# A blocked forward substitution turned the other way round: one 32 by 32 product for each pair of blocks, three sets per slot instead of four

## The chip, the core and the metric

The kernel runs on one core of one Trainium2 chip. The metric is the device time of one execution in microseconds (us), given as the median of several executions. All executions told of here are on record as in the fast state. A ratio between two kernels is the mean time of one kernel's fast runs over the mean of the other's of the same rounds, so it is not quite the ratio of the medians that are quoted.

## The reference

Attention of the delta-rule kind for 4 batches, 8 heads, 768 tokens and 48 columns a head; its output, brought to 3072 rows of 384, goes through an MLP of 2048 hidden columns. Everything is fp32. `beta` is between 0.1 and 0.4.

```python
k_n = k / (np.linalg.norm(k, axis=-1, keepdims=True) + 1e-06)
for t in range(S):
    kt, vt, bt = (k_n[:, :, t], v[:, :, t], beta[:, :, t, None])
    y[:, :, t] = np.einsum('bhd,bhde->bhe', q[:, :, t], state)
    v_old = np.einsum('bhde,bhd->bhe', state, kt)
    state = state + bt[:, :, :, None] * np.einsum('bhd,bhe->bhde', kt, vt - v_old)
...
x = np.ascontiguousarray(attn_out.transpose(0, 2, 1, 3)).reshape(B * S, H * D)
h = x @ w_in
return (h * (1.0 / (1.0 + np.exp(-1.702 * h)))) @ w_out
```

## The kernel before

The 768 steps are done in 6 chunks of 128 tokens, so that there are 24 *units*, one for each chunk and batch. In a unit, the values that the state really takes up (U) come from a lower triangular system of 128 rows for each head. It is solved in four blocks of 32 rows. The diagonal blocks have been inverted beforehand by VectorE (XB). Block b is then `U[b] = XB[b] * (V[b] - sum over a < b of G[a,b]^T U[a])`, where V holds the values and G comes from the products of the unit's keys with each other. The kernel forms each sum by *one* product over all blocks above, so its rows of the array are 32, 64 or 96, and calls it psR:

```python
def keys(self):                      # V -= what the state holds for these keys
    ...
    psK = [bank("psK", (128, NP, D)) for _ in range(2)]
    ...                              # 8 products
    for hh in range(2):
        Vh = self.V[:, hh::2, :]
        vec.tensor_tensor(Vh, Vh, psK[hh], op=ALU.subtract)

def above(self, blk, h, psR):
    r, a = slice(blk * BS, (blk + 1) * BS), slice(0, blk * BS)
    pe.matmul(psR[r, h, :], lhsT=self.G[a, h, 0, r], rhs=self.U[a, h, :], start=True, stop=True)

def rest(self, blk, psR):            # VectorE
    r = slice(blk * BS, (blk + 1) * BS)
    vec.tensor_tensor(self.V[r], self.V[r], psR[r], op=ALU.subtract)

def solve(self, blk, h, psU):
    r = slice(blk * BS, (blk + 1) * BS)
    pe.matmul(psU[r, h, :], lhsT=self.XB[r, h, :], rhs=self.V[r, h, :], start=True, stop=True)

def solved(self, blk, psU):          # ScalarE
    r = slice(blk * BS, (blk + 1) * BS)
    act.copy(self.U[r], psU[r])
```

`slot(n)` works on three units at once, A (unit n-1), B_ (unit n) and D_ (unit n+1), in six groups. Between the groups it puts MLP matmuls (ph, po), which need nothing from these units and fill TensorE. psR, psU, psK, psY (queries and outputs) and psS (state) come from one pool of four PSUM buffers, which `bank` hands out in turn:

```python
if group == 0:    psR of A, block 2
elif group == 1:  psU of A, block 2, mixed head by head with psR of B_, block 1
elif group == 2:  psR of A, block 3;  D_ begins: D_.keys()
elif group == 3:  psU of A block 3, B_ block 1, D_ block 0;  A.queries()
elif group == 4:  A.state()
else:             A.outputs()
# after each group: some instructions of the inversion (VectorE), weight conversion, MLP
```

(The cases are told in words here; the code is in the diff below.)

## Time and profile before

| | before |
|---|---|
| time, median of 3 (range) | 853.62 us (852.58 to 853.96) |
| span of the profiled execution | 851.5 us |
| TensorE busy | 93% |
| VectorE busy | 57% |
| sets of substitution products in a steady slot | 4 (16, 32, 16 and 48 matmul records) |
| one steady slot | 31.1 us |

The main views stand in the prediction. What it does not show are the page's groups of the instructions that the change touches. The columns are line, engine, operation, output and inputs, shapes and count; then busy time in us and mean ns of one; then the engine's idle time ahead of them and what ended it.

```profile
L529 DVE TENSOR_TENSOR V<-V,psR 32x384 f32<-32x384 f32 x68 | 37.6, 553 | 92.5 <-PE psR L522 91.4
L522 PE MATMUL psR<-US,G 64*32 64x48 f32 (+2 forms) x1088 | 60.8, 207 | 0.0
L533 PE MATMUL psU<-V,XB 32*32 32x48 f32 x1424 | 42.5, 204 | 2.3 <-DVE V L529 2.3
```

The "+2 forms" are the products over 32, 64 and 96 rows. The mean of 207 ns is the length of one record; the 1088 of them make 60.8 us of busy time, so they overlap for the most part, and 207 ns is not what one costs. A group is not complete either, because the first slots' instructions carry the line of a helper.

### The profile page before, as it was taken

How to read it: one execution, taken by the hardware profiler on the slowest of the kernel's cores; microseconds unless marked ns; L12 is line 12 of the kernel's file. 1: busy time of each engine (PE TensorE's matmuls, PEld its weight loads, DVE VectorE, ACT ScalarE, POOL GpSimd, SP SyncE). 2: the span in 40 equal slices, each digit the busy share in tenths (PEclk: the TensorE clock that was granted, in tenths of full speed). 3: DMA queues.
4: the chain of work that ended last, by engine and by line, in shares of the span. 5: the costliest groups of instructions: out<-in, count | busy, mean ns of one | idle time of the engine just before them, and what ended most of it. 6: DMA issues, size and time to landing. Idle time of an engine off the chain costs nothing.

```text
span 851.5 us, 16186 instructions
## 1 busy us (share of the span) xinstructions
PE 794.0 (93%) x6884; PEld 578.7 (68%) x6884; DVE 483.2 (57%) x1025; ACT 200.8 (24%) x383; POOL 106.0 (12%) x120
## 2 busy tenths in 40 slices
PE   8308898899999999999999999999999999999998
PEld 7206677656766867867767767767767768677684
DVE  5799869978993592582682672772762840110100
ACT  3202544232311312312212312213212112112020
POOL 2102321231021202102102101101100000000000
PEclk9658969999999999999999999999999999999999
DMA  9798653451322213223122132032032020000000
GB/s 150 157 158 152 162 143 81 112 142 34 77 59 58 60 42 73 54 64 69 36 66 68 36 85 57 18 86 54 10 79 52 1 58 2 10 15 1 24 1 18
DMA packets 160967, 55.80 MB, mean 66 GB/s; under 512 B 128672, under 2 KB 157568, under 8 KB 160896
## 3 DMA queue, kind: packets, MB, share of 16 engines
q1 hardware_dynamic: 154048, 46.02, 26.6%
q0 software_dynamic: 1856, 7.87, 3.0%
q10 hardware_dynamic: 4992, 0.89, 0.9%
q8 instruction: 54, 0.88, 0.4%
q14 instruction: 17, 0.14, 0.1%
HBM read 33.13 MB, written 20.45 MB: 63 GB/s over the span
## 4 chain that ended last, share of the span: by engine, by line
PE 78%; DVE 12%; DMA 6%; issue 2%; POOL 1%; ACT 0%; ACTq 0%; SPq 0%; DVEq 0%; POOLq 0%
PE po L629 28%; PE ph L614 27%; PE psG L368 4%; PE psR L522 4%; PE psY L549 4%; PE psU L533 4%; PE psK L512 2%; DVE P L104 2%; DMA w_out<-in_moe_w_out_dram 2%; PE psT L354 2%; DVE YB L104 1%; DMA w_out<-in_moe_w_in_dram 1%; PE psS L571 1%; DMA QP<-in_q_dram 1%; PE ps_warm L104 1%
## 5 line engine op out<-in xcount | busy, mean ns | idle before, releaser
L614 PE MATMUL ph<-xT,w_in 128*128 128x256 f32 (+1 forms) x1248 | 273.7, 373 | 2.8 <-ACT gT L619 1.9
L629 PE MATMUL po<-w_out,gT 128*128 128x384 f32 x768 | 269.4, 497 | 1.9 <-DVE w_out L194 1.8
L614 PEld LDWEIGHTS ph<-xT,w_in 128*128 128x128 f32 x1248 | 221.2, 194 | 41.7 <-issue 11.2
L629 PEld LDWEIGHTS po<-w_out,gT 128*128 128x128 f32 x768 | 140.8, 191 | 95.2 <-issue 9.5
L619 ACT ACTIVATE gT<-ph 128x512 f32<-128x512 f32 (+1 forms) x104 | 58.5, 563 | 193.8 <-PE ph L614 193.7
L529 DVE TENSOR_TENSOR V<-V,psR 32x384 f32<-32x384 f32 x68 | 37.6, 553 | 92.5 <-PE psR L522 91.4
L540 ACT COPY US<-psU 32x384 f32<-32x384 f32 x89 | 41.8, 469 | 140.8 <-PE psU L533 81.7
L522 PEld LDWEIGHTS psR<-US,G 64*32 64x32 f32 (+2 forms) x1088 | 51.0, 109 | 19.7 <-issue 18.4
L368 PE MATMUL psG<-kqT 48*128 48x256 f32 x352 | 55.5, 419 | 7.1 <-DVE G L376 4.4
L522 PE MATMUL psR<-US,G 64*32 64x48 f32 (+2 forms) x1088 | 60.8, 207 | 0.0
L392 POOL TENSOR_SCALAR_AFFINE_SELECT G<-G 128x1024 f32<-128x1024 f32 x24 | 27.2, 1132 | 247.0 <-DVE G L376 155.4
L154 PE MATMUL ps_warm<-ident 128*128 128x256 bf16 x152 | 22.1, 312 | 35.1 <-DVE ps_warm L104 32.8
L636 DVE COPY o<-po 128x384 f32<-128x384 f32 x24 | 13.3, 555 | 72.9 <-PE po L629 72.7
L533 PEld LDWEIGHTS psU<-V,XB 32*32 32x32 f32 x1424 | 35.0, 105 | 25.4 <-issue 12.7
L432 DVE TENSOR_TENSOR P<-NT,YB 64x2 f32<-64x2 f32 (+4 forms) x135 | 46.6, 345 | 4.1
L436 DVE TENSOR_REDUCE YB<-P 64x2 f32<-64x2 f32 (+4 forms) x135 | 43.3, 321 | 4.4
L533 PE MATMUL psU<-V,XB 32*32 32x48 f32 x1424 | 42.5, 204 | 2.3 <-DVE V L529 2.3
L372 ACT ACTIVATE G<-psG 128x512 f32<-128x512 f32 x44 | 26.3, 598 | 75.1 <-PE psG L368 74.0
L154 PEld LDWEIGHTS <-ident 128*128 128x128 bf16 x152 | 16.7, 112 | 39.7 <-DVE ps_warm L104 33.5
L368 PEld LDWEIGHTS psG<-kqT 48*128 48x128 f32 x352 | 34.2, 197 | 13.5 <-DVE G L376 4.8
L590 DVE COPY last<-psY 128x128 f32<-128x128 f32 x20 | 5.7, 287 | 53.7 <-PE psY L549 53.7
L304 POOL TENSOR_TENSOR ksq<-KN 128x384 f32<-128x384 f32 x17 | 14.6, 856 | 172.3 <-DMA KN<-in_k_dram 172.3
(115 smaller groups left out, 732.8 us busy)
## 6 DMA issues: line engine op xcount, KB each, us to landing
Nd<-G SPq DMA_DIRECT2D x24, 512.0 KB, 3.2
w_out<-in_moe_w_out_dram POOLq DMA_DIRECT2D x14, 384.0 KB, 3.9
KN<-in_k_dram SPq DMA_DIRECT2D x24, 192.0 KB, 3.3
V<-in_v_dram SPq DMA_DIRECT2D x24, 192.0 KB, 3.2
out_dram<-o SPq DMA_DIRECT2D x24, 192.0 KB, 1.9
QP<-in_q_dram SPq DMA_DIRECT2D x20, 192.0 KB, 2.9
w_out<-in_moe_w_in_dram SPq DMA_DIRECT2D x6, 576.0 KB, 12.4
NT<-Nd SPq DMA_DIRECT2D x24, 128.0 KB, 2.5
```

The lines of the kernel that those rows point to most:

```text
L104: return lambda *a, **kw: tc.keep_in_program_order(op(*a, **kw))
L154: pe.matmul(ps, lhsT=ones[:, 0:128], rhs=ones, start=True, stop=True)
L368: pe.matmul(ps[hh][:, i], lhsT=kqT[pr, g + i, 0, :], rhs=kqT[pr, g + i, :, :], start=True, stop=True,)
L432: tt(P, diag(Nf, i * BS, [[0, i], [1, i]]), diag(Yf, 0, [[BS, i], [1, i]]), op=ALU.mult,)
L436: red(diag(Yf, i, [[BS, i]]), P, axis=AX.X, op=ALU.add, negate=True)
L522: pe.matmul(psR[r, h, :], lhsT=self.G[a, h, 0, r], rhs=self.U[a, h, :], start=True, stop=True,)
L529: vec.tensor_tensor(self.V[r], self.V[r], psR[r], op=ALU.subtract)
L533: pe.matmul(psU[r, h, :], lhsT=self.XB[r, h, :], rhs=self.V[r, h, :], start=True, stop=True,)
L540: act.copy(self.U[r], psU[r])
L614: pe.matmul(ph[:, u], lhsT=w_in[:, j, f * 128 : (f + 1) * 128], rhs=xT[:, j, t], start=(j == 0), stop=(j == KC - 1),)
L619: act.activation(gT[f0 // FQ][:, f0 % FQ : f0 % FQ + 2, t], ph, ACT.Gelu_apprx_sigmoid)
L629: pe.matmul(po, lhsT=gT[f // FQ][:, f % FQ, i * C : (i + 1) * C], rhs=w_out[:, f, :], start=(f == 0), stop=(f == FC - 1),)
```

## The change

The sums are done the other way round. As soon as block b of U is known, its part in *every later* block is formed, each by its own product of 32 rows by 32 columns (`below`), and subtracted at once. There are more products, 6 per head and unit instead of 3, but all have the same small shape and lie in different tiles of the array. A unit now needs no set of its own between two solves: in one set, some units are solved while others' blocks are passed on. Three sets are left per slot. Queries and outputs also move together, and the state follows the third set.

```diff
-        def above(self, blk, h, psR):
-            r, a = slice(blk * BS, (blk + 1) * BS), slice(0, blk * BS)
-            pe.matmul(
-                psR[r, h, :], lhsT=self.G[a, h, 0, r], rhs=self.U[a, h, :],
-                start=True, stop=True,
-            )
+        def below(self, blk, h, psR):
+            r = slice(blk * BS, (blk + 1) * BS)
+            for k in range(blk + 1, NB):
+                u = slice(k * BS, (k + 1) * BS)
+                pe.matmul(
+                    psR[u, h, :], lhsT=self.G[r, h, 0, u], rhs=self.U[r, h, :],
+                    start=True, stop=True,
+                )
 
         def rest(self, blk, psR):
-            r = slice(blk * BS, (blk + 1) * BS)
-            vec.tensor_tensor(self.V[r], self.V[r], psR[r], op=ALU.subtract)
+            for u in (slice(BS, 2 * BS), slice(2 * BS, C)) if blk == 0 else (slice((blk + 1) * BS, C),):
+                vec.tensor_tensor(self.V[u], self.V[u], psR[u], op=ALU.subtract)
... new: together(solves, belows), which takes a psU and a psR buffer and issues,
... head by head, every solve and every below of the set, then the copies and subtractions
             if group == 0:
-                ... psR of A, block 2
                 next(P, None)
                 next(P, None)
             elif group == 1:
-                ... psU of A, block 2, with psR of B_, block 1
+                together([(B_, 1)], [(A, 2)])
                 next(P, None)
             elif group == 2:
-                ... psR of A, block 3
                 ... D_.keys()
             elif group == 3:
-                ... psU of A block 3, B_ block 1, D_ block 0
+                together([(A, 3), (D_, 0)], [(B_, 1)])
+            elif group == 4:
                 if A:
                     A.queries()
-            elif group == 4:
+                    A.outputs()
+            else:
+                together([(B_, 2)], [(D_, 0)])
                 if A:
                     A.state()
-            elif A:
-                A.outputs()
```

More of the change, by code (lines that the diff above doesn't have):

```diff
@@ L676, with together @@
     steps, xTs, inverting, gT0 = {}, {}, iter(()), []
+    def together(solves, belows):
+        solves = [(X, blk) for X, blk in solves if X]
+        belows = [(X, blk) for X, blk in belows if X]
+        psU = bank("psU") if solves else None
+        psR = bank("psR") if belows else None
+        for h in range(H):
+            for X, blk in solves:
+                X.solve(blk, h, psU)
+            for X, blk in belows:
+                X.below(blk, h, psR)
+        for X, blk in solves:
+            X.solved(blk, psU)
+        for X, blk in belows:
+            X.rest(blk, psR)
     def slot(n, share):
@@ L692, in slot @@
             if group == 0:
-                if A:
-                    psR = bank("psR")
-                    for h in range(H):
-                        A.above(2, h, psR)
-                    A.rest(2, psR)
                 next(P, None)
@@ L700, in slot @@
             elif group == 1:
-                psU = bank("psU") if A else None
-                psR = bank("psR") if B_ else None
-                for h in range(H):
-                    if A:
-                        A.solve(2, h, psU)
-                    if B_:
-                        B_.above(1, h, psR)
-                if A:
-                    A.solved(2, psU)
-                if B_:
-                    B_.rest(1, psR)
+                together([(B_, 1)], [(A, 2)])
                 next(P, None)
             elif group == 2:
-                if A:
-                    psR = bank("psR")
-                    for h in range(H):
-                        A.above(3, h, psR)
-                    A.rest(3, psR)
                 if n + 1 < len(units):
@@ L726, in slot @@
             elif group == 3:
-                psU = bank("psU")
-                turns = [(X, blk) for X, blk in ((A, 3), (B_, 1), (D_, 0)) if X]
-                for h in range(H):
-                    for X, blk in turns:
-                        X.solve(blk, h, psU)
-                for X, blk in turns:
-                    X.solved(blk, psU)
+                together([(A, 3), (D_, 0)], [(B_, 1)])
+            elif group == 4:
                 if A:
                     A.queries()
-            elif group == 4:
+                    A.outputs()
+            else:
+                together([(B_, 2)], [(D_, 0)])
                 if A:
                     A.state()
-            elif A:
-                A.outputs()
             next(K, None)
```

## The prediction

> **What bounds the kernel now.** I read the page's busy shares and slices first, then the busy times by stretch, then the chain of work that ended last, and then the starts of single instructions. The page:
>
> ```profile
> PE 794.0 (93%) x6884; PEld 578.7 (68%) x6884; DVE 483.2 (57%) x1025; ACT 200.8 (24%) x383; POOL 106.0 (12%) x120
> ...
> PE   8308898899999999999999999999999999999998
> ...
> DVE  5799869978993592582682672772762840110100
> ...
> PEclk9658969999999999999999999999999999999999
> ```
>
> TensorE is full from about slice 11 to the end. Before that VectorE is as full as TensorE, and the granted clock dips. The stretches (TensorE, its weight loads, VectorE, ScalarE, GpSimd, then clock and DMA share) say where the border lies:
>
> ```profile
> 140.00:180.00 40.00, 36.86 (x352) 28.60 (x351) 35.25 (x67) 13.95 (x30) 10.22 (x12) 0.94 0.54 126
> ...
> 200.00:240.00 40.00, 38.07 (x349) 29.92 (x350) 38.05 (x80) 12.81 (x24) 3.86 (x4) 1.00 0.27 61
> 240.00:300.00 60.00, 60.00 (x551) 43.21 (x551) 34.98 (x76) 12.77 (x24) 11.65 (x10) 1.00 0.27 60
> ```
>
> From about 233 us, where slot 6 begins, TensorE never stops. A slot takes 31.1 us, and what a slot costs is the sum of its TensorE pieces. The chain over one slot has only TensorE in it (start, length, piece); I show the attention pieces and leave the MLP between them out:
>
> ```profile
> 511.44 0.80 PE psR L522 x16
> 512.23 1.02 PE psT L354 x8
> ...
> 517.92 0.01 PE psR L522
> 517.93 1.06 PE psG L368 x8
> ...
> 523.08 0.80 PE psR L522 x16
> 523.87 1.03 PE psK L512 x16
> ...
> 529.91 0.81 PE psU L533 x48
> 530.72 0.60 PE psY L549 x16
> ```
>
> The substitution appears four times: psR of block 2 at 511.44, the mixed psU/psR set from 517.13 to 517.93, psR of block 3 at 523.08, and the psU set of three units at 529.91. Each takes 0.80 or 0.81 us, though they hold 16, 32, 16 and 48 matmul records (every fp32 product has two records, so 8 heads give 16). The time of a set does not depend on how many products are in it. The starts of the single instructions tell why: in a set that uses one tile of the array the starts are 42.5 ns apart and the set runs 662 ns from first start to last; with two tiles a second record follows each by 7 ns, 668 ns; with three tiles, 675 ns. So one tile takes a 48-column record every 42.5 ns, another tile's record comes 7 ns behind it, and a set lasts 16 rounds. At its edges lie borders: from one MLP matmul (ph) to the next is 216 ns, but from ph to a set's first record 309 ns, so 93 ns more; from the last record to the next piece is 131 to 136 ns instead of 42.5, so about 90 more.
>
> [...] The change puts up to three products on one row group[...]. Before has no 32-row set with a shared row group, but has wider ones. The queries (psY, 48 rows by 64 columns, two tiles on each row group) start four records 7 ns apart and the next four 109 ns later, which is the round of one tile: the outputs, 128 columns streamed on two tiles, have the same 109. The state (psS, all 128 rows, two column tiles) has a round of 58 ns. [...] the trace has the loads of two column tiles on the same rows side by side. I take the independence to hold for 32 rows and three tiles also.
>
> **The change part by part.**
>
> 1. Products. Before: 24 psR and 32 psU per unit. After: 48 psR (blocks 0, 1, 2 give three, two, one for each head) and 32 psU, so 192 more products over 24 units, times 3: 576 products or 1152 records more. By the rounds above they cost nothing if each head's products lie in different tiles. They do: (block rows, output quadrant) is (1,1),(2,3) in the first set; (3,3),(0,0),(1,2),(1,3) in the second; (2,2),(0,1),(0,2),(0,3) in the third. Each tile is still used 16 times, so a set stays at 16 rounds, 682 ns of starts with four tiles (662 + 3 x 7).
>
> 2. Sets. In a steady slot three instead of four. The compiled order of the changed kernel shows them whole: psR8+psU8, psR16+psU16, psR24+psU8 in every slot from the seventh on. Queries and outputs now touch, the third set touches the state, and psT stands by itself between full-array matmuls. I count the borders between modes in a slot: 16 before, 14 after. First start to last start, the sets took 662 + 668 + 662 + 675 = 2667 ns, and would take 668 + 682 + 682 = 2032: 635 ns less. To this come the last round of the set that goes, 42.5, and two borders of 91: 0.86 us per slot.
>
> 3. How many slots. Slots 6 to 23 have TensorE full: 18 x 0.86 = 15.5 us. The last slot (only one unit left) goes from four sets to two and from 11 borders to 7: 2 x 0.70 + 4 x 0.09 = 1.8 us. Two mixed sets of before are broken up by MLP matmuls, at 265 us (pieces of 204, 282, 283 and 459 ns, 1228 instead of 799) and at 699 us (197 + 283 + 629, 1109 instead of 799); after has no broken set from slot 6 on: 0.43 + 0.31 = 0.74 us. Sum of the steady part: 18.0 us.
>
> 4. VectorE. The subtraction of psR from V is three instructions per unit before (32x384, 552 ns by its group's row) and four after. Rows should not matter: the copy of po, 128x384, takes 555 ns. So 24 x 0.55 = 13 us more VectorE, all hidden from 233 us on, where it is at most 26 of 31 us busy in a slot. ScalarE's copies stay at four per unit.
>
> 5. The first 233 us. Three sets fewer fall here, 2.4 us of TensorE. But it waits there anyway: I add up 14.8 us of longer waits between 76 and 240 us, of which two are psU waiting for V (2.0 us at 91, 2.2 us at 151). The new order leaves two groups of MLP work, not one, between a subtraction and the solve that needs it, which could take these waits away. Against it, VectorE gets about six more subtractions, 3.3 us, where it is 76 to 95% busy, and several early sets of the changed kernel are broken up in the order. I put the net at 1.5 us saved, a guess with 4 us on each side.
>
> Sum: 18.0 + 1.5 = 19.5; 853.6 - 19.5 = 834.1 us, 2.3% faster.
>
> **The rivals.**
>
> *Products on one row group queue up.* Then the second set has 32 records on row group 1 and the third 48 on row group 0: 16 rounds of 85 and of 127.5 ns, 0.68 and 1.36 us more. Per slot +2.04 - 0.86 = +1.2, over 24 slots +28: 882 us. For it: no 32-row case in the trace[...]. Against: queries, outputs and state. I give it 6%.
>
> *Only the weight loads queue up.* [...] the state speaks against it. 9%.
>
> *The start becomes the bound.* VectorE's extra work, a sooner wait of VectorE on psR in its fixed order there, or another dip of the clock (0.83 between 100 and 140 us) could lengthen the first 233 us, and all later work with it: the full steady gain, but 838 to 842 us. Equally it could lose its two waits and the clock dip and end at 829.
>
> *VectorE or ScalarE late in the steady part.* A set now waits on values from two groups earlier, instead of one, with 5 to 10 us of MLP between[...]. And the PSUM buffers: 11 allocations a slot over four buffers instead of 10, but psY is held for one group instead of two. I expect no new wait.
>
> **Range and chances.** Without a rival (85%) I expect 834.1 with some 4 us on each side from the start; the border of 2% is at 836.5, close by, so about two thirds of that lies under it. The range for 8 in 10: 829 to 842. Faster by over 2%: 0.59; within 2%: 0.32; slower: 0.09.
>
> **What would show it.** A steady slot of 30.25 us instead of 31.1. Sets of about 0.81 us with 32, 64 and 64 records, in rounds of 42.5 ns[...]. psS right behind the third set, queries and outputs as one piece. About 24 more VectorE subtractions, those with 64 rows at 0.55 us. Slot 6 beginning within 4 us of 233. It is wrong if the third set is longer than the first, if slots have new TensorE waits, or if slot 6 starts much later.

## The result, and the profile after

The changed kernel takes 840.0 us, the median of four runs (839.97 to 845.1), beside 853.1 us before (850.8 to 853.96). The ratio is 0.9865, with a 95% interval of 0.9824 to 0.9907. It is faster by a little over 1.3%, inside the predicted range of 829 to 842, but 6 us above the predicted time, and so within 2% and not beyond it.

The page of the changed kernel, in the same lines as those of before in the prediction (busy times and counts, then the slices of TensorE, VectorE and the granted clock):

```profile
PE 780.8 (93%) x8036; PEld 569.2 (68%) x8036; DVE 489.2 (58%) x1049; ACT 200.3 (24%) x383; POOL 109.8 (13%) x120
...
PE   8307789999899999999999999999999999999998
...
DVE  5698779978977484584584592692781851110000
...
PEclk9657879999899999999999999999999999999999
```

TensorE has 1152 records more and is busy for 13 us less. The stretch in which it is full looks the same, except for one dent in slice 11, in which the clock has one too. The stretches by time say where it lies (TensorE, weight loads, VectorE, ScalarE, GpSimd, then clock and DMA share):

```profile
140.00:180.00 40.00, 39.66 (x453) 29.39 (x452) 38.16 (x72) 13.97 (x31) 10.26 (x13) 1.00 0.55 127
200.00:240.00 40.00, 36.93 (x335) 28.72 (x328) 32.82 (x71) 10.82 (x20) 4.97 (x4) 0.91 0.27 58
240.00:300.00 60.00, 60.00 (x656) 43.73 (x655) 39.33 (x81) 13.96 (x27) 11.79 (x10) 1.00 0.29 63
```

From 240 us on TensorE is full, as before. Between 140 and 180 us it is fuller than before (39.66 instead of 36.86 us). Between 200 and 240 us it is less full (36.93 instead of 38.07), and the clock is at 0.91 instead of 1.00.

The chain of work that ended last shows what a steady slot is now made of (start, length, piece). It splits the mixed sets into single records; I show their first and last pieces:

```profile
525.65 0.16 PE psU L535 x2
...
526.46 4.08 PE ph L616 x18
530.54 1.62 PE psY L551 x32
532.16 2.79 PE ph L616 x12
534.95 0.15 PE psU L535
535.11 0.02 PE psR L524 x3
...
535.75 0.02 PE psR L524 x3
535.77 0.60 PE psS L573 x16
```

The second set runs from 525.65 to 526.46, which is 0.81 us for 64 records. The third runs from 534.95 to 535.77, 0.82 us for 64 records, three psR on the same row group for each psU. Queries and outputs are one piece of 32 records, and the state follows the third set without MLP between. From first start to last start the three sets take 668, 682 and 682 ns, as predicted, and the same set comes again every 30.2 us (at 495.37, 525.58, 555.80 and 586.00 us).

The groups of the changed instructions:

```profile
L531 DVE TENSOR_TENSOR V<-V,psR 32x384 f32<-32x384 f32 x87 | 48.3, 556 | 91.5 <-PE psR L524 89.6
L535 PE MATMUL psU<-V,XB 32*32 32x48 f32 x1408 | 60.5, 204 | 0.0
L524 PE MATMUL psR<-US,G 32*32 32x48 f32 x2080 | 58.2, 203 | 0.0
```

A subtraction on 64 rows costs no more than one on 32: the 44 with 32 rows and the 43 with 64 in this group all took 547 to 561 ns. VectorE's 6 us more are paid nowhere in the steady part, but for one wait of 0.4 us at 335 us, in which MLP matmuls wait for a copy by VectorE.

To see where the gain went, I took the start times of three single MLP matmul records, which are the same 2016 records in the same order in every kernel: the first, the 288th and the 384th (counted from 0). The last column has the stretches after 200 us, and before the very end, in which the granted TensorE clock was one half.

| kernel | first record | 288th | from 288th to 384th | from 384th to the end | half clock after 200 us (start, length) |
|---|---|---|---|---|---|
| before | 115.6 | 209.5 | 41.3 | 600.7 | none |
| after | 119.2 | 208.4 | 45.9 | 584.0 | 226.0, 6.8 |

The steady part (from the 384th on) is shorter by 16.8 us. The stretch before it, some 41 us that contain slot 5, is longer by 4.6 us. The rest of the start is 1.1 us shorter. Together that is -13.3 us, the difference of the spans.

What happens in slot 5 is in the timelines. First TensorE, before (start, length, line, shapes, count; in brackets the wait and what ended it):

```profile
217.48 0.65 PE L549 MATMUL psY<-kqT,ST 48*64 48x128 f32 x8
218.06 3.29 PE L614 MATMUL ph<-xT,w_in 128*128 128x256 f32 x14
222.85 0.65 PE L549 MATMUL psY<-kqT,ST 48*64 48x128 f32 x8 [1.50 <-DVE V L518]
```

And after:

```profile
218.96 0.65 PE L551 MATMUL psY<-kqT,ST 48*64 48x128 f32 x8
219.54 1.56 PE L616 MATMUL ph<-xT,w_in 128*128 128x256 f32 x6
224.18 0.65 PE L551 MATMUL psY<-kqT,ST 48*64 48x128 f32 x8 [3.07 <-DVE V L518]
224.76 1.77 PE L616 MATMUL ph<-xT,w_in 128*128 128x256 f32 x6
226.46 0.60 PE L535 MATMUL psU<-V,XB 32*32 32x48 f32 x5
```

The second half of the queries waits in both, for the subtraction of psK (line 518) on VectorE, since its PSUM buffer is one of those that psK had. VectorE before:

```profile
222.44 0.35 DVE L518 TENSOR_TENSOR V<-V,psK 128x192 f32<-128x192 f32 x1
222.82 1.22 DVE L466 TENSOR_TENSOR YS<-YB,bI 64x1024 f32<-64x1024 f32 x1
224.08 0.35 DVE L518 TENSOR_TENSOR V<-V,psK 128x192 f32<-128x192 f32 x1
```

And after:

```profile
217.39 0.35 DVE L518 TENSOR_TENSOR V<-V,psK 128x192 f32<-128x192 f32 x1
...
221.64 2.09 DVE L416 TENSOR_REDUCE YB<-P 64x64 f32<-64x768 f32 x2
223.76 0.35 DVE L518 TENSOR_TENSOR V<-V,psK 128x192 f32<-128x192 f32 x1
```

Here VectorE works off an inversion in its compiled order and reaches the *second* subtraction at about 224 us in both kernels. Before, the queries went on after the first one; after, they go on only after the second. By the order of the `bank` calls this is the work of the new sets: psR of the mixed set now takes a buffer between psK and psY, so that the second psY falls on the buffer of the second psK. TensorE comes to this wait at nearly the same time in both kernels (221.35 and 221.11 us: the first half of the queries starts 1.5 us later, with less MLP behind it), but it is let go 1.3 us later. So the wait is 3.07 us instead of 1.50, and 1.8 us after it the clock halves for 6.8 us, in which MLP matmuls start 427 ns apart instead of 216; so about half of it is lost. The extra 1.57 us and 3.4 us explain the 4.6 us, less what the new sets already save there. Half clock comes in multiples of 3.4 us here (6.8 us, and twice 3.4 us in the kernel before, at 154.7 and 178.6 us). What sets it off was not shown: in the two stretches of 3.4 us ahead of 226.0 us TensorE was idle for 1.46 and for 1.61 us.

### The profile page after: what moved, and what is told of

It reads as the page before. It is cut to its first block, busy times and chain, and to the rows that moved or that the text cites. A ratio compares the mean times of both kernels' runs of the same rounds, so it can differ in the third digit from the quotient of the medians.

```text
span 838.2 us, 18516 instructions
## 1 busy us (share of the span) xinstructions
PE 780.8 (93%) x8036; PEld 569.2 (68%) x8036; DVE 489.2 (58%) x1049; ACT 200.3 (24%) x383; POOL 109.8 (13%) x120
## 4 chain that ended last, share of the span: by engine, by line
PE 74%; DVE 12%; DMA 7%; issue 3%; POOL 2%; SPq 1%; ACT 0%; ACTq 0%; DVEq 0%; POOLq 0%
PE po L631 28%; PE ph L616 27%; PE psG L368 4%; PE psU L535 4%; PE psY L551 4%; DMA w_out<-in_moe_w_out_dram 2%; PE psK L512 2%; DVE P L104 2%; PE psR L524 2%; PE psT L354 1%; DMA w_out<-in_moe_w_in_dram 1%; DMA QP<-in_q_dram 1%; DVE YB L104 1%; DVE w_in L104 1%; PE psS L573 1%
## 5 line engine op out<-in xcount | busy, mean ns | idle before, releaser
L616 PEld LDWEIGHTS ph<-xT,w_in 128*128 128x128 f32 x1248 | 221.7, 194 | 39.8 <-issue 9.3
L531 DVE TENSOR_TENSOR V<-V,psR 32x384 f32<-32x384 f32 x87 | 48.3, 556 | 91.5 <-PE psR L524 89.6
L542 ACT COPY US<-psU 32x384 f32<-32x384 f32 x88 | 41.3, 469 | 166.4 <-PE psR L524 148.1
L535 PEld LDWEIGHTS psU<-V,XB 32*32 32x32 f32 x1408 | 50.5, 106 | 30.2 <-issue 21.1
L535 PE MATMUL psU<-V,XB 32*32 32x48 f32 x1408 | 60.5, 204 | 0.0
L524 PE MATMUL psR<-US,G 32*32 32x48 f32 x2080 | 58.2, 203 | 0.0
L638 DVE COPY o<-po 128x384 f32<-128x384 f32 x24 | 13.3, 555 | 75.4 <-PE po L631 75.1
L524 PEld LDWEIGHTS psR<-US,G 32*32 32x32 f32 x2080 | 49.1, 105 | 1.0 <-issue 0.7
L307 DVE TENSOR_REDUCE ssq<-ksq 128x8 f32<-128x384 f32 x17 | 9.4, 550 | 47.1 <-POOL ksq L304 47.1
```

The lines of the kernel that those rows point to most:

```text
L524: pe.matmul(psR[u, h, :], lhsT=self.G[r, h, 0, u], rhs=self.U[r, h, :], start=True, stop=True,)
L531: vec.tensor_tensor(self.V[u], self.V[u], psR[u], op=ALU.subtract)
L616: pe.matmul(ph[:, u], lhsT=w_in[:, j, f * 128 : (f + 1) * 128], rhs=xT[:, j, t], start=(j == 0), stop=(j == KC - 1),)
```

## The experiments

Ten runs are on record, all of them correct and in the fast state. The kernel before ran beside each. A median does not tell everything here, since single executions of one kernel differ by 5 us and more; so I read each run's trace by the stretches above as well; a trace is of one execution, too.

**The old form in the start.** Slots below 6 keep the old form, slot 6 is mixed (old psR of A, and `below` of B_'s block 0), and from slot 7 on everything is as in the changed kernel.

```diff
+            old, mid = n < 6, n == 6
             ...
-                together([(B_, 1)], [(A, 2)])
+                if old: ... as in the kernel before
+                elif mid: together([(A, 2), (B_, 1)], [])
+                else: together([(B_, 1)], [(A, 2)])
             ... (the other groups likewise)
```

> The start in the form of before, the new form from slot 6 on (slot 6 itself is a mixture with an extra set). Theory 1 (the steady part gains all that was predicted, the start of the changed kernel gives about 5 us back): early part as before (MLP record 384 starts at about 251 us, not 254), steady slots 30.25 us, end at 853.1 - 16.5 + 0.8 for the extra set of slot 6, about 837 us, 3 us faster than the changed kernel. Theory 2 (the start is no worse in the changed kernel; the steady part gains less than predicted): 840 us or more.

It took 837.05 us (835.97 to 839.96), ratio 0.9822 (0.9797 to 0.9847), against 852.62 of before in the same call. From the 384th record to the end it needed 583.2 us, 17.5 less than before; from the 288th to the 384th, 41.8 us, about what before needs. The wait of the queries is short again:

```profile
222.28 0.65 PE L562 MATMUL psY<-kqT,ST 48*64 48x128 f32 x8 [1.49 <-DVE V L518]
```

So the steady gain holds by itself, and what is lost is lost before it. No version has a lower median, though the one with the border at slot 2 (below) is no slower within the noise.

**The stall of VectorE at 82 us.** In the changed kernel VectorE stands still for 6.86 us at 82.3 us, waiting for psR of the first unit, while weight conversions wait behind it. This edit spreads the conversions of slot 0 in another way over its groups.

```diff
-            more = left // (GR - group)
+            more = (1, 1, 0, 0, 0, 1)[group] if n == 0 else left // (GR - group)
```

> The changed kernel, with two weight conversions of slot 0 moved ahead of the subtraction at 89 us, for which VectorE stands idle 6.9 us. Theory 1a (this stall sets the start back by the 3.7 us by which the first MLP matmul comes later): the first MLP matmul at about 116 us instead of 119, end at 836 to 838 us. Theory 1b (the stall is hidden: VectorE waits for GpSimd's power until 125.0 us in both kernels, and the set-back comes later, at 221 us): end within 1 us of 840.

It took 840.45 us (838.35 to 843.01), ratio 0.9858 (0.9832 to 0.9884), so no difference from the changed kernel; the profiled execution was its fastest. The 6.9 us wait is split into two, 4.7 us in sum. The first MLP record comes 1.6 us earlier (117.6) and the 288th as well (206.8), but the wait in slot 5 (3.2 us) and half clock after it (3.4 us) are there again. The stall is not where the time is lost.

**One block's products twice.** The products of block 2 are done twice, into the same place, so the first set has 32 records on one tile instead of 16.

```diff
-            for k in range(blk + 1, NB):
+            for k in list(range(blk + 1, NB)) * (2 if blk == 2 else 1):
```

> The changed kernel with each product of block 2 issued twice into the same tile, same result: 8 more products per unit (16 records), a sixth of those of the run with free tiles. If a tile's rounds set a set's time: the first set of each slot 32 rounds instead of 16, 0.68 us longer, 24 x 0.68 = 16 us in all, about 855 us. If the time goes by the number of products: 16 records of 7 ns, 3 us in all.

It took 863.21 us (856.8 to 864.84), ratio 1.0104 (1.0067 to 1.0141). The first set ran 1348 ns from first start to last instead of 668, in 32 rounds, and a steady slot took 30.9 us instead of 30.2. So in this set the records *of one tile* made the time, as the prediction took it. From the 384th record on it needed 14.1 us more than the changed kernel. The other 10 us of the difference came before: the clock was at half for 20.5 us from 180.4 us on in the profiled execution. The fastest run, 856.8, lies near what the steady part alone would make of it.

**Products into free tiles too.** Every block is passed on to all four blocks; the results that are not wanted are not read. This was to show whether four products on one row group queue up.

```diff
-            for k in range(blk + 1, NB):
+            for k in range(NB):
```

> The changed kernel with all four products for each block, also into quadrants of the bank that nobody reads: 48 more products per unit (96 records), 1152 in all, all into tiles that are free. Results stay right. If a tile costs only its 7 ns of issue behind the others: sets of 16 rounds of 42.5 ns still, 5 or 6 tiles, 690 to 696 ns from first start to last, some 0.04 us more per slot, about 1 us in all (841). If products on one row group share anything: rounds longer than 42.5 ns, at 6 tiles 0.1 to 1.4 us more per set and 10 to 80 us in all.

It took 866.5 us (865.56 to 870.26), ratio 1.0170 (1.0143 to 1.0198): a miss of the 841 us, and within what was expected if products on one row group share something. Rounds were indeed longer than 42.5 ns, but the row group alone does not fit. The sets of five tiles (80 records) ran 754 ns and those of six (96 records) 886 ns from first start to last. The stretches of the second and of the third set, in time:

```profile
486.33:487.35 1.02, 1.02 (x97) 0.96 (x97) 0.00 (x0) 0.01 (x1) 0.00 (x0) 1.00 0.01 1
495.84:496.72 0.88, 0.88 (x82) 0.81 (x84) 0.78 (x4) 0.62 (x2) 0.00 (x0) 1.00 0.00 0
```

Both sets have four products on one row group, but they differ in time as they do in records: 886 / 96 = 9.2 ns and 754 / 80 = 9.4 ns a record. So a queue on the row group does not explain them, and a cost for each record would; what lies behind that was not shown. An estimate from these two sets: with four tiles a round would need 4 x 9.3 = 37 ns, less than the 42.5 ns of one tile; with five 47 and with six 55. That fits the changed kernel, which has up to four and whose sets with four still ran 682 ns; a fifth tile did cost something. The longer sets make 0.36 us per slot (86 + 204 + 72 ns), some 6.5 us over the 18 slots of the steady part. That part is 20.7 us longer in all: waits of TensorE for 7.0 us and half clock for 10.2 us in two stretches, half of it lost if it went as in slot 5 of the changed kernel, make most of the rest; another 6.0 us were lost before the 384th record. Why these waits came I did not follow up.

**The changed kernel once more**, as a base for the next three runs on the same chip.

> The changed kernel once more, on the chip of the next two, as their base: 840 us, with the wait of TensorE before psY at 221 us (3.1 us) and the half clock after it (6.8 us) in the profile. If both are there again they belong to the kernel and not to one execution.

It took 840.83 us (840.27 to 841.38), ratio 0.9859 (0.9844 to 0.9873). The wait in slot 5 is 3.3 us, with half clock of 3.4 us after it (6.8 us was expected), and the stretch from the 288th to the 384th record takes 44.4 us.

**The queries in other buffers.** The PSUM buffers of the queries come from another pool in the first two chunks, so that they do not wait for psK's.

```diff
-            self.psY = [bank("psY", (128, 2, 128)) for _ in range(2)]
+            self.psY = [
+                ps_big.tile([128, 2, 128], F32, tag="big", name="psY") if self.c < 2 else bank("psY", (128, 2, 128))
+                for _ in range(2)
+            ]
```

> The changed kernel with psY of the first two row chunks (slots 1 to 8) in the two buffers of psT and psG instead of the four that it shares with psK, psR and psU. Theory 2a (in the new order both psY take the buffers that the two psK of the same slot have just left, so that TensorE waits at 221 us for the second subtraction on VectorE, and its clock then halves): wait and half clock gone, MLP record 384 at 250 to 251 us, end at 835.5 to 837. Theory 2b (VectorE is simply late, and the solve of the next unit needs the same subtraction): the wait moves to psU a few us later and the end is 838 to 840.

It took 842.48 us (840.92 to 844.2), ratio 0.9879 (0.9860 to 0.9897), no gain. The queries no longer wait, but the next set does:

```profile
225.36 0.86 PE L535 MATMUL psU<-V,XB 32*32 32x48 f32 x15 [3.99 <-DVE V L531]
```

The solves need the V that VectorE only has after its second subtraction of psK and one of psR. So the buffer is merely the first thing to show that VectorE is late. In the new order TensorE asks for its values too soon in this slot, with too little MLP in between. In the kernel before, 7.2 us lie between the second half of the queries and the solves (222.85 and 230.1 us); in the changed kernel it is 2.3 us (224.18 and 226.46).

**Help for VectorE.** Two multiplications of the inversion in the second chunk, each done twice there (1.22 us on VectorE), go to GpSimd, in the changed kernel and in the one with the old start.

```diff
-        tt(N, N, bc, op=ALU.mult)
+        (nc.gpsimd.tensor_tensor if c == 1 else tt)(N, N, bc, op=ALU.mult)
...
-        vec.tensor_tensor(YS, Y, bc, op=ALU.mult)
+        (nc.gpsimd if c == 1 else vec).tensor_tensor(YS, Y, bc, op=ALU.mult)
```

> The changed kernel with the scaling of N and of the inverse by beta for the second row chunk on GpSimd, four instructions of 1.2 to 1.3 us less on VectorE, three of them before 224 us. If VectorE's lateness at 224 us is what TensorE waits for (2a and 2b alike): the wait before psY shrinks by up to 3 us and the clock stays up, 835 to 838. If the start is held by something else (DMA of w_out, GpSimd's power): no change, or later[...]: 840 to 842.

> The old start with the new form from slot 6, and the four instructions on GpSimd as well. The waits before psU at 150 us (3.2 us) and before psY at 220 us (1.6 us) of the run with the old start are for VectorE too: up to 3 us less than its 837, 834 to 836. If VectorE isn't what holds the start: 837.

They took 842.31 us (840.88 to 843.25), ratio 0.9871 (0.9854 to 0.9887), and 838.79 us (838.34 to 839.18), ratio 0.9835 (0.9820 to 0.9849): by the medians 1.5 us and 1.7 us slower than the same kernels without the edit (the second of which ran in another call). The 288th record comes late (211.5 and 212.2 us), and in the first of them the wait of 3.3 us is still there. But the edit was hardly a test of slot 5. In the trace of the changed kernel with it, the four instructions run on GpSimd at 116, 158, 162 and 226 us, for 1.90 to 2.22 us each. Without it, the one nearest to slot 5's wait stood at 224.15 us on VectorE, just *behind* the second subtraction. So VectorE was relieved of nothing in the 60 us before that subtraction, which came at 225.84 us. Whether relief there would help stays open.

**Where in the start.** The same edit as in the first experiment, but with the border at slot 2 or at slot 4.

```diff
-            old, mid = n < 6, n == 6
+            old, mid = n < 2, n == 2        # in the other kernel: n < 4, n == 4
```

> The old form in slots -1 to 1, a mixed slot 2, the new form from slot 3. It asks which slots of the start give back what the steady part gains. Theory A (the place is slot 5, where the second subtraction of psK comes late and the clock then halves): this kernel still has the new form in slots 4 and 5, so it ends like the changed kernel, 840 us (839 to 842), with a TensorE wait near 220 us of about 3 us and a half-clock window after it. Theory B (the loss is made in the first slots, -1 to 2, and slot 5 only passes it on): this kernel ends like the one with the old form up to slot 6, 837 us (836 to 838.5), with the 384th MLP record near 251 us.

> The old form in slots -1 to 3, a mixed slot 4, the new form from slot 5. Theory A (slot 5 is the place): 840 us (839 to 842), with the wait of about 3 us near 220 us and a half-clock window after it, as slot 5 is still in the new form. Theory B (the first slots make the loss): 837 us (836 to 838.5), the 384th MLP record near 251 us. If this run shows 837 and the one that changes over at slot 2 shows 840, the place lies in slots 2 to 4.

The first took 837.3 us (836.19 to 838.91), ratio 0.9806 (0.9777 to 0.9834), the second 839.3 us (836.35 to 839.58), ratio 0.9821 (0.9790 to 0.9853); before ran at 853.06 in this call, but from 851.4 to 858.69. By the final time, theory A fits the second and theory B the first. The traces are clearer. Both have the wait (3.3 and 4.1 us) and half clock after it (3.4 and 6.8 us), as A said and B did not. The kernels by the same stretches as above, without the two that have extra records:

| kernel | form in slot 5 | wait before psY or psU near 220 us | 288th | from 288th to 384th | from 384th to the end | half clock near 225 us |
|---|---|---|---|---|---|---|
| before | old | 1.5 | 209.5 | 41.3 | 600.7 | none |
| old start to slot 6 | old | 1.5 | 208.9 | 41.8 | 583.2 | none |
| the same, GpSimd helps | old | 1.2 | 212.2 | 40.5 | 584.1 | none |
| after | new | 3.1 | 208.4 | 45.9 | 584.0 | 6.8 |
| after once more | new | 3.3 | 209.2 | 44.4 | 584.6 | 3.4 |
| old start to slot 2 | new | 3.3 | 207.4 | 44.5 | 583.7 | 3.4 |
| old start to slot 4 | new | 4.1 | 207.5 | 46.6 | 583.4 | 6.8 |
| VectorE's stall spread | new | 3.2 | 206.8 | 44.4 | 585.3 | 3.4 |
| queries in other buffers | new | 4.0 | 207.3 | 44.4 | 587.9 | 3.4 |
| GpSimd helps | new | 3.3 | 211.5 | 44.5 | 585.6 | 3.4 |

With the old form in slot 5 the stretch takes 40.5 to 41.8 us, with the new one 44.4 to 46.6, whatever the slots before it are. The two with extra records have the new form too, and fit in: waits of 3.0 us (twice the products) and 3.9 us (free tiles; there for a DMA of XB), half clock after or in them, and 44.9 and 44.8 us for the stretch. So the place of the loss is shown: it is slot 5. The final times also depend on when the 288th record is reached, which differs by 5 us between these kernels. Why the kernel with the border at slot 2 gets there 2 us before the kernel of before, and so ends at 837 in spite of its wait, is not settled. The one with the border at slot 4 gets there as early (207.5) and then loses 2.1 us more, with a longer wait and 6.8 us of half clock instead of 3.4. The long last stretch of the kernel with other buffers holds one more stretch of half clock (3.4 us from 277.2 us on).

## Why the prediction was right or wrong

*Products (step 1): right.* 1152 records more cost nothing, in rounds of 42.5 ns, with three products on one row group (682 ns for the set). The rival of products that queue up fell: rounds of 85 or 127 ns were not seen. Nor were weight loads seen to queue up: in the third set, at 535.3 us, those on one row group start 6 to 7 ns apart and take 105 ns each, side by side like those of the state's two column tiles (6 to 7 ns apart, 133 to 138 ns each). The run with a tile used twice shows that the busiest tile counts (1348 ns for 32 rounds). The run with free tiles adds what the step did not know: sets grew to 754 and 886 ns with a fifth and a sixth tile, some 9.3 ns a record, so that four tiles, by my estimate from these two, are just within the round. The 7 ns between two tiles were no measure of how many fit.

*Sets and slots (steps 2 and 3): right, a little too large.* The sets ran 668, 682 and 682 ns, and the slot 30.2 us. From the 384th record on 16.8 us were gained (17.5 us with the old start), instead of 18.0 from the beginning of slot 6. About half of slot 6, 0.4 us, lies before that record, and one new wait of 0.4 us stands in the steady part of the changed kernel, MLP matmuls waiting for a copy by VectorE.

*VectorE (step 4): right.* 24 more instructions, and those with 64 rows take about 0.55 us. Summed over the trace, the helper's among them, the subtractions of psR took 53.3 us (96) instead of 39.8 (72), so 13.5 us more, as the step said. VectorE's busy time on the page grew by only 6.0 us, because other instructions took less, above all 44 products of the inversion (P<-NT, 37.0 instead of 41.5 us); why they did is not traced. The new ones are hidden from slot 6 on.

*The first 233 us (step 5): wrong.* The step put "the net at 1.5 us saved, a guess with 4 us on each side". In its place came 3.5 us lost up to the 384th record: 1.1 us saved up to the 288th, and 4.6 us lost in slot 5. Of the two waits for V that the step hoped to remove, the one at 151 us is gone (TensorE 39.66 instead of 36.86 us busy between 140 and 180 us), and the other is still there (2.3 us up to 96.0 us, instead of 1.9). The step's sum of waits, 14.8 us, is 14.4 in the list of the trace, which changes nothing. But the step looked only at what stands between a subtraction and its solve. It did not look at what stands between VectorE's late subtractions of psK and the queries and solves that come after them, and there the new order ties the queries to the second subtraction and leaves less MLP before the solves. The sentence on buffers, "I expect no new wait", fails at the same place: not in the steady part, but in slot 5, where VectorE is late. And half clock for 6.8 us followed the wait, for which the step had no term. The rival "the start becomes the bound", at 838 to 842 us, is what came, by a dip of the clock, which it had named, after a wait, and not by VectorE's extra instructions.

The sum: 5.0 us from the start (3.5 lost instead of 1.5 gained) and 1.2 us from the steady part turn 19.5 us into the 13.3 us of the spans. The sign that I had named, slot 6 beginning within 4 us of 233 us, was ill chosen: the new slot 5 ends only after the third set and the state, so it is at 240 us, while the MLP work is 3.5 us behind.

## What to carry to other kernels

Small products in tiles that are free in a round cost nothing here with up to four tiles (682 ns a set), and something with five and six (754 and 886 ns); measure that number by adding one more tile before counting on it. When TensorE's sets get fewer and move together, check in each slot where another engine is late how much independent work still lies between its results and their users, and not only in the steady part. A wait of TensorE cost more than its length here: in slot 5 half clock came after or in every wait of 3.0 us or more (3.4 or 6.8 us of it in the table above; in the changed kernel MLP matmuls then started 427 ns apart instead of 216), and with none of 1.5 us or less. Elsewhere the length of one wait did not tell: the clock halved after single waits of 2.28 us (kernel before, at 154 us) and 1.02 us (products twice, at 180 us), and once with only 0.46 us of idle time in the 3.4 us ahead of it (queries in other buffers, at 277.2 us), but not right after one of 1.91 us at 93 us in the kernel before. What decides is open.
